# Soft-capped attention for two heads at a time in half-array tiles, with fp32 values and the softmax denominators summed on VectorE

## The chip, the cores and the metric

One core of one Trainium2 chip runs the whole program. The metric is the device time of one execution in microseconds (us). In what follows PE is TensorE, DVE is VectorE, ACT is ScalarE, POOL is GpSimd, and SP is the engine that issues nearly all DMAs.

## The reference

Three layers run one after the other on 4 batches of 448 tokens (12 heads of 64, model width 768):

```python
scores = scale * q @ k.T                       # per head, 448 x 448
scores = cap * np.tanh(scores / cap)
attn = np.exp(scores - max); attn /= attn.sum(-1)
x = (attn @ v)                                 # heads side by side: 1792 x 768
h = x @ w_in                                   # 768 -> 2048, weights given as 64-bit floats
x = (h * np.clip(h + 3, 0, 6) / 6) @ w_out     # 2048 -> 768
# then a top-1 mixture of 8 experts (768 -> 1024 -> 768) with a gate and an output gate
```

All of it is wanted to fp32 accuracy.

## The kernel before

One order of work is written for every engine by a small planner (class `Work`): each step is recorded with its engine, a due time `at`, an assumed duration and the buffers that it uses; `run()` then plays the steps through a list schedule and emits them in the order that it finds. The engines follow that order strictly, each its own, whatever the real times are. DMAs are steps of the engine "sp".

The stages in the order of time: attention of batch 0, with the conversion of the 64-bit weights beside it (`cv`, lines 392 to 446: load, four integer steps on DVE, store to a scratch array); then three stages in each of which the feed-forward layer (`step`, line 640) of batch b runs on PE, and the attention of batch b+1 is woven between its matmuls; the feed-forward layer of batch 3; the experts. In the first of these three stages the rest of the conversion runs too. At the end of each feed-forward layer `route` (line 756) picks the experts, POOL scatters token numbers with four indirect DMAs (line 833, `order<-ids,posi`), and `rows` (line 862) transposes the layer's output back and writes it with the DMA `xs<-spare` (line 885).

Attention is recorded head by head (`head`, line 479). q and k are turned by four PE transposes each pair of key chunks (line 492). ACT copies them out as fp32r, a format that PE multiplies in one pass (line 505); DVE subtracts to get the rounding rests (lines 509, 511). High part and rest lie in different halves of the 128 array rows, so that two matmuls per key chunk give all the products that are kept (lines 554, 555). For this the halves are doubled by two DMAs within the chip per head (line 516, `qk<-qk`; for the first four heads by copies on DVE or ACT). ACT takes tanh (line 561) and exp (line 568). The values:

- heads 0 to 15 (`nat`): one fp32 matmul per key chunk (line 582), shown in the trace as two records;
- the others: exp is split in a high part and a rest (line 300 or 298, and line 575), and three fp32r matmuls per key chunk follow (lines 586 to 588).

In both cases POOL copies v into a wider tile whose other 64 columns are ones (lines 532, 537, 540), so that the same matmul gives the denominators in the other 64 output rows. Four ACT copies per pair of heads bring values and denominators to the right halves (line 600), DVE divides (lines 617 to 625).

The buffers that couple the engines: two tiles each for q2, k2, v2, loaded by SP (line 462); the load of v waits until POOL has copied the older v out. Two raw weight tiles `wr` and three split ones `ws`; two row tiles `spare` for `rows`. PSUM: S0, S1 (two banks each) for scores, T for transposes, U (and F1 in batch 0) for values, F0, F1 for the feed-forward layer.

## Time and profile before

| | us |
|---|---|
| median of 3 runs | 1168.71 (1166.28 to 1173.0) |
| the profiled execution | 1165.38 |
| its span, first to last instruction | 1163.7 |
| attention of batch 0 and feed-forward 0 with attention 1, up to the first routing | 0 to 285 |
| feed-forward 1 with attention 2, up to the second routing | 285 to 480 |
| feed-forward 2 with attention 3, up to the third routing | 480 to 661 |
| feed-forward 3, up to the last routing | 661 to 805 |
| experts | 805 to 1164 |

The ends of the stages are the starts of the routing matmuls (line 778): six fp32 matmuls with 32 output columns each, which stand at four column positions of the array in turn (0, 32, 64, 96, 0, 32), two records each. The page's first part gives each engine's busy time, the second the same by 40 slices of 29 us; the windows give it by stage. A matmul's duration in a record overlaps that of the next one; what one costs in a stream is the distance between two starts.

### The profile page before, as it was taken

Reading aid. Unit: us, or ns where it says so; the run is one execution under the profiler, and the core shown is the slowest. Engines: PE = TensorE matmul, PEld = TensorE weight load, DVE = VectorE, ACT = ScalarE, POOL = GpSimd, SP = SyncE. Lnnn points to the kernel's source line nnn. Section 1 sums busy time; section 2 is a strip of 40 time slices with the busy share of each in tenths; the row PEclk is TensorE's granted clock in tenths of the full one; section 3 lists DMA queues with packets and bytes.
Section 4 is the critical chain, followed back from the end, with each engine's and each line's share of the span. In section 5 each row is a group of like instructions: output and inputs, shape, how many; then the busy total and the mean of one; then the engine's idle time right before and its main releaser. Section 6 shows DMA issues by size and latency. Waiting matters only on the chain.

```text
span 1163.7 us, 17177 instructions
## 1 busy us (share of the span) xinstructions
PE 1067.8 (92%) x5416; PEld 879.7 (76%) x5416; DVE 789.2 (68%) x1317; ACT 763.2 (66%) x1056; POOL 138.5 (12%) x209
## 2 busy tenths in 40 slices
PE   6879999999989999949999987999849999999995
PEld 3446888888879999739999876998746667886764
DVE  6879898997854676726587562444927776886662
ACT  7889877986855886836687352434726766886663
POOL 2001001111120010110013002000171100110001
PEclk9999999999989999979999999999979999999998
DMA  8888888884763443334333287345356868949562
GB/s 246 254 248 237 263 251 250 258 264 128 133 113 113 113 130 95 85 76 143 94 94 102 68 170 205 120 129 211 89 180 220 304 217 310 351 164 333 171 187 82
DMA packets 123985, 209.43 MB, mean 180 GB/s; under 512 B 14010, under 2 KB 82474, under 8 KB 123888
## 3 DMA queue, kind: packets, MB, share of 16 engines
q1 hardware_dynamic: 120304, 197.22, 57.6%
q0 software_dynamic: 3584, 11.04, 2.7%
q8 instruction: 45, 0.74, 0.3%
q14 instruction: 52, 0.43, 0.1%
HBM read 224.20 MB, written 25.83 MB: 215 GB/s over the span
## 4 chain that ended last, share of the span: by engine, by line
PE 50%; DMA 16%; DVE 13%; issue 13%; ACT 4%; POOL 2%; SPq 1%; POOLq 0%; DVEq 0%
PE F L636 8%; PE F L634 8%; PE F L635 8%; PE S L634 5%; PE S L636 4%; PE S L635 4%; DMA order<-ids,posi 4%; DMA xs<-spare 3%; DMA f<-in_moe_w_in_dram 2%; PE F L1387 2%; PE S L554 2%; PE S L555 2%; DVE ws L663 2%; PE U L587 1%; PE U L586 1%
## 5 line engine op out<-in xcount | busy, mean ns | idle before, releaser
L663 DVE TENSOR_TENSOR ws<-wr,ws 128x768 fp32r<-128x768 f32 (+1 forms) x112 | 119.4, 1068 | 75.1 <-ACT ws L660 73.9
L660 ACT ACTIVATE ws<-wr 128x768 fp32r<-128x768 f32 (+1 forms) x112 | 104.2, 931 | 47.6 <-DMA wr<-wsi 24.0
L634 PE MATMUL F<-gT,ws 128*128 128x448 f32 x320 | 119.0, 372 | 1.2 <-ACT ws L660 1.2
L636 PE MATMUL F<-gT,ws 128*128 128x448 f32 x320 | 117.9, 368 | 2.0 <-DVE ws L663 2.0
L635 PE MATMUL F<-gT,ws 128*128 128x448 f32 x320 | 117.1, 366 | 0.0
L561 ACT ACTIVATE S<-S,rcap 112x896 f32<-112x896 f32 x96 | 93.5, 976 | 26.9 <-PE S L555 26.3
L575 DVE TENSOR_TENSOR el<-et,eh 112x896 fp32r<-112x896 f32 x64 | 70.1, 1095 | 24.9 <-ACT eh L300 24.1
L634 PE MATMUL S<-ring,hTm 128*128 128x384 f32 x224 | 83.7, 374 | 0.0
L554 PE MATMUL S<-qk 128*112 128x448 f32 x192 | 80.2, 417 | 1.1 <-DMA qk<-qk 1.0
L634 PE MATMUL F<-xTb,ws 128*128 128x448 f32 x192 | 73.7, 384 | 4.6 <-DVE r L690 3.9
L635 PE MATMUL S<-ring,hTm 128*128 128x384 f32 x224 | 76.4, 341 | 1.1 <-DVE ring L1258 1.1
L636 PE MATMUL S<-ring,hTm 128*128 128x384 f32 x224 | 76.2, 340 | 0.0
L634 PE MATMUL F<-xTa,ws 128*128 128x448 f32 x192 | 74.6, 389 | 1.7 <-DVE r L690 1.2
L1258 DVE TENSOR_TENSOR ring<-w2B,ring 128x768 fp32r<-128x768 f32 x56 | 52.6, 956 | 29.4 <-ACT ring L1254 26.4
L1258 DVE TENSOR_TENSOR ring<-w2A,ring 128x768 fp32r<-128x768 f32 x56 | 52.9, 956 | 28.5 <-ACT ring L1254 27.7
L555 PE MATMUL S<-qk 128*112 128x448 f32 x192 | 71.8, 374 | 0.0
L636 PE MATMUL F<-xTb,ws 128*128 128x448 f32 x192 | 70.8, 369 | 0.0
L635 PE MATMUL F<-xTa,ws 128*128 128x448 f32 x192 | 70.8, 369 | 0.0
L636 PE MATMUL F<-xTa,ws 128*128 128x448 f32 x192 | 70.7, 368 | 0.0
L635 PE MATMUL F<-xTb,ws 128*128 128x448 f32 x192 | 70.7, 368 | 0.0
L1254 ACT ACTIVATE ring<-w2B 128x768 fp32r<-128x768 f32 x56 | 46.9, 846 | 34.9 <-PE S L636 32.3
L568 ACT ACTIVATE et<-S,capt 112x896 f32<-112x896 f32 x64 | 64.4, 1007 | 7.5 <-DVE el L575 6.3
(269 smaller groups left out, 2723.3 us busy)
## 6 DMA issues: line engine op xcount, KB each, us to landing
wr<-wsi SPq DMA_DIRECT2D x64, 384.0 KB
wr<-wso SPq DMA_DIRECT2D x48, 512.0 KB
w1A<-in_moe_w_dram SPq DMA_DIRECT2D x42, 512.0 KB
w2A<-in_moe_w_dram SPq DMA_DIRECT2D x56, 384.0 KB
w1B<-in_moe_w_dram SPq DMA_DIRECT2D x42, 512.0 KB
w2B<-in_moe_w_dram SPq DMA_DIRECT2D x56, 384.0 KB
spare<-in_moe_w_dram SPq DMA_DIRECT2D x72, 256.0 KB
spare<-in_moe_w_dram SPq DMA_DIRECT2D x96, 192.0 KB
```

What stands on the lines that cost most here:

```text
L554: nc.tensor.matmul(out=sp[:P, j, 0:S], lhsT=k1f[:, c], rhs=qsf, start=True, stop=False)
L555: nc.tensor.matmul(out=sp[:P, j, 0:S], lhsT=kkf[:, c], rhs=qsf, start=False, stop=True)
L561: lambda sv=sv: A.activation(out=sv, in_=sv, func=ACTF.Tanh, scale=rcap[:P]), [s] + caps, [hs])
L568: lambda sv=sv, hx=hx: A.activation(out=hx.t, in_=sv, func=ACTF.Exp, scale=capt[:P]), [s], [hs, hx])
L575: lambda e=e, he=he, el=el: V.tensor_tensor(out=el, in0=e, in1=he.t.bitcast(F32), op=ALU.subtract),
L634: nc.tensor.matmul(out=acc, lhsT=lh, rhs=rh, start=first, stop=False)
L635: nc.tensor.matmul(out=acc, lhsT=lh, rhs=rl, start=False, stop=False)
L636: nc.tensor.matmul(out=acc, lhsT=ll, rhs=rh, start=False, stop=last)
L660: lambda: A.activation(out=s[:, 0, 0:n], in_=t, func=ACTF.Copy), [x], [hw, hs])
L663: lambda: V.tensor_tensor(out=s[:, 1, 0:n], in0=t, in1=s[:, 0, 0:n].bitcast(F32), op=ALU.subtract),
L1254: "act", at - 5e3, 40 + w * 0.887, lambda: A.activation(out=hs.t[:, 0, 0:w], in_=raw(), func=ACTF.Copy),
L1258: lambda: V.tensor_tensor(out=hs.t[:, 1, 0:w], in0=raw(), in1=hs.t[:, 0, 0:w].bitcast(F32), op=ALU.subtract),
```

## The change

`head(g)` becomes `pair_qk(n)` and `pair(n)`, for two heads that stand in the two halves of the array.

- q, k, v are loaded with the two heads side by side in each key chunk (pieces of 64 numbers, 256 bytes, where there were 256 numbers); a transpose then turns both heads at once. One ACT copy and one DVE subtraction for each of q and k.
- Scores: three products (high x high, high x rest, rest x high), each as two matmuls, one per head, on 64 array rows each and into banks of their own: six instructions per key chunk and pair, where there were four.
- The doubling of halves is gone, with its DMAs and copies.
- Values in fp32 for all heads: per key chunk two matmuls of 64 output columns, one per head, into the two halves of one bank. v is read as it was loaded; POOL has no part in it.
- Denominators: DVE adds the four exp tiles of a pair (three additions of 112x896), and two fp32 matmuls with ones follow. The high part, rest and copy of exp are gone.
- One ACT copy of the denominators per pair; DVE's division reads the values from PSUM.
- In batch 0 transposes take T and F0 in turn; from batch 1 on scores are recorded for two key chunks at a time.
- The planner's due times: T0 88 to 70, T1 188 to 174, conversions every 4.4 where it was 5.5; six feed-forward matmuls are assumed to take 1225 ns where it was 1125.

```diff
@@ -274,7 +262,7 @@
-    nc.gpsimd.iota(tokid, pattern=[[1, 2], [2, 2]], base=0, channel_multiplier=C, allow_small_or_imprecise_dtypes=True)
+    nc.gpsimd.iota(tokid, pattern=[[1, C]], base=0, channel_multiplier=C, allow_small_or_imprecise_dtypes=True)
...
     Sp, Tp, Up, F, U2 = banks("S0", "S1"), banks("T"), banks("U"), banks("F0", "F1"), banks("U", "F1")
+    T2 = banks("T", "F0")
     TU, Y3 = banks("T", "U"), banks("S0a", "S0b", "S1a", "S1b")
-    QKV = {nm: ring(atp, 2, [P, 2, C, D], nm) for nm in ("q2", "k2", "v2")}
-    QK = ring(atp, 2, [128, 3, 2, 2 * P], "qk", F32R)
-    ET = ring(atp, 1, [P, 2, S], "et")
-    EH = Tag(atp, 3, [P, 2, S], "eh")
-    EL = ring(atp, 2, [P, 2, S], "el", F32R)
+    QKV = {nm: ring(atp, 2, [P, C, 2, D], nm) for nm in ("q2", "k2", "v2")}
+    QK = ring(atp, 2, [128, 2, 2, S], "qk", F32R)
+    EE = ring(atp, 7, [P, 2, S], "ee")
+    ES = ring(atp, 1, [P, 2, S], "es")
...
-    for par in range(2):
...
-    T0, T1, TL = 88e3, 188e3, 120e3
+    T0, T1, TL = 70e3, 174e3, 120e3
...
-        at = i * 5.5e3 if i < 16 else max(T0, t_ff(i // 2) - 30e3)
+        at = i * 4.4e3 if i < 16 else max(T0, t_ff(i // 2) - 30e3)
...
@@ -459,166 +432,137 @@
-                nc.sync.dma_start(
-                    out=h.t.rearrange("p h c d -> p h (c d)"),
-                    in_=src[b, 2 * p:2 * p + 2].rearrange("h (p c) d -> p h (c d)", c=C),
-                )
+                nc.sync.dma_start(out=h.t, in_=src[b, 2 * p:2 * p + 2].rearrange("h (p c) d -> p c h d", c=C))
...
+    def pair_qk(n):
         b, p = divmod(n, H // 2)
...
+        t0, per = t_head(2 * n), (t_head(2 * n + 2) - t_head(2 * n)) / 2
+        load(n)
+        (hq, lq), (hk, lk) = (loaded[n, nm] for nm in ("q2", "k2"))
+        TR = T2 if b == 0 else Tp
+        hw = QK.take()
+        w = hw.t
+        ready = []
+        for i, (h, l) in enumerate(((hq, lq), (hk, lk))):
+            ht = TR.take()
+            def trans(tp=ht.t, t=h.t):
+                for c in range(C):
+                    nc.tensor.transpose(tp[:, c * P:(c + 1) * P], t[:, c].rearrange("p h d -> p (h d)"), ident[:P, :P])
+            at = t0 - 1.6 * per + i * 500
+            tt = ht.t[:, 0:S]
+            x = work.add("pe", at, 392, trans, [l], [ht, h], rows=P)
+            x = work.add(
+                "act", at + 1e3, 467, lambda i=i, tt=tt: A.activation(out=w[:, i, 0], in_=tt, func=ACTF.Copy),
+                [x], [ht, hw])
+            ready.append(work.add(
+                "dve", at + 1e3, 535,
+                lambda i=i, tt=tt: V.tensor_tensor(
+                    out=w[:, i, 1], in0=tt, in1=w[:, i, 0].bitcast(F32), op=ALU.subtract),
+                [x], [ht, hw]))
+        turned_qk[n] = hw, ready
+    def pair(n):
+        b, p = divmod(n, H // 2)
+        t0, per = t_head(2 * n), (t_head(2 * n + 2) - t_head(2 * n)) / 2
+        hv, lv = loaded[n, "v2"]
+        hw, ready = turned_qk[n]
+        w = hw.t
+        TR, UR = (T2, U2) if b == 0 else (Tp, Up)
+        hu, hsum = UR.take(), ES.take()
+        uv, es = hu.t, hsum.t
+        many = 1 if b == 0 else 2
+        et, last = [], None
+        for c0 in range(0, C, many):
+            at = t0 + c0 * per / 2
+            hs = [Sp.take() for _ in range(many)]
+            def score(c0=c0, hs=hs):
+                for c, h in enumerate(hs):
+                    for t, (i, j) in enumerate(((0, 0), (0, 1), (1, 0))):
+                        for r in range(2):
+                            o = slice(64 * r, 64 * r + 64)
+                            nc.tensor.matmul(
+                                out=h.t[:P, r, 0:S], lhsT=w[o, 1, i, (c0 + c) * P:(c0 + c + 1) * P], rhs=w[o, 0, j],
+                                start=(t == 0), stop=(t == 2))
+            s = work.add("pe", at - 0.8 * per, 200 + 612 * many, score, ready, hs + [hw])
+            for c, h in enumerate(hs):
+                sv = h.t[:P, :, 0:S]
+                x = work.add(
+                    "act", at - 4e3 + c * 2e3, 900,
+                    lambda sv=sv: A.activation(out=sv, in_=sv, func=ACTF.Tanh, scale=rcap[:P]), [s] + caps, [h])
+                he = EE.take()
+                x = work.add(
+                    "act", at - 3e3 + c * 2e3, 900,
+                    lambda sv=sv, he=he: A.activation(out=he.t, in_=sv, func=ACTF.Exp, scale=capt[:P]), [x], [h, he])
+                et.append((he, x))
+                k = len(et) - 1
+                if k == 0:
+                    continue
+                one = et[0][0] if k == 1 else hsum
+                last = work.add(
+                    "dve", at - 2e3 + c * 2e3, 1002,
+                    lambda he=he, one=one: V.tensor_tensor(out=es, in0=one.t, in1=he.t, op=ALU.add),
+                    [et[0][1], x, last], [he, one, hsum] if k == 1 else [he, hsum])
+        hd = TR.take()
+        dv = hd.t
+        def pv(c0):
+            for c in range(c0, c0 + 2):
+                for r in range(2):
+                    nc.tensor.matmul(
+                        out=uv[64 * r:64 * r + 64, 0:S], lhsT=hv.t[:, c, r], rhs=et[c][0].t[:, r],
+                        start=(c == 0), stop=(c == C - 1))
+        def total():
+            for r in range(2):
+                nc.tensor.matmul(out=dv[64 * r:64 * r + 64, 0:S], lhsT=ones[:, 0:64], rhs=es[:, r], start=True, stop=True)
+        x = None
+        for c0 in range(0, C, 2):
+            hes = [et[c][0] for c in (c0, c0 + 1)]
+            if c0 + 2 < C:
+                x = work.add(
+                    "pe", t0 + c0 * per / 2, 1700, lambda: pv(0), [et[0][1], et[1][1], lv], [hu, hv] + hes, rows=P)
             else:
...
+                x = work.add(
+                    "pe", t0 + c0 * per / 2, 2450, lambda c0=c0: (pv(c0), total()), [x, et[2][1], et[3][1], last],
+                    [hu, hv, hd, hsum] + hes, rows=P)
+        hx, hy, hr, hc, xt = UX.take(), US.take(), RT.take(), RC.take(), XT[b % 2].take()
         ux, us, rt, rc, x2 = hx.t, hy.t, hr.t, hc.t, xt.t
         nb = S // 32
 
         def blocks(t):
             return t.rearrange("p (n w) -> p n w", w=32)
 
...
+        at = min(t0 + 2.5 * per, T0 + b * T1 - 6e3 + p * 500)
+        pe = x
+        x = work.add("act", at, 467, lambda: A.activation(out=us, in_=dv[:, 0:S], func=ACTF.Copy), [pe], [hd, hy])
+        x = work.add("dve", at, 535, lambda: V.transpose(out=blocks(rt), in_=blocks(us)), [x], [hy, hr])
         x = work.add("dve", at, 160, lambda: V.reciprocal(out=rc, in_=blocks(rt)[:, :, 0:1]), [x], [hr, hc])
         x = work.add(
             "dve", at, 535, lambda: V.transpose(out=blocks(us), in_=rc.to_broadcast([128, nb, 32])), [x], [hc, hy])
...
+        x = work.add(
+            "dve", at, 535, lambda: V.tensor_tensor(out=ux, in0=uv[:, 0:S], in1=us, op=ALU.mult), [x, pe], [hu, hx, hy])
         x = work.add(("dve", "act"), at, (302, 467), copier(x2[:, 0], ux), [x], [hx, xt])
         x = work.add(
             "dve", at, 535,
...
-                "pe", t0 + m / n * (t1 - t0), 1125, mm, [ws, last, xs_[m][1], xs_[m + 1][1]],
+                "pe", t0 + m / n * (t1 - t0), 1225, mm, [ws, last, xs_[m][1], xs_[m + 1][1]],
...
-    plan = [(t_head(g) if g else -1, lambda g=g: head(g)) for g in range(NH)]
-    plan += [(i * 5.5e3 if i < 16 else t_ff(i // 2) - 30e3, lambda i=i: cv(i)) for i in range(len(parts))]
+    plan = [(t_head(2 * n - 2) - 1 if n else -2, lambda n=n: pair_qk(n)) for n in range(NH // 2)]
+    plan += [(t_head(2 * n) if n else -1, lambda n=n: pair(n)) for n in range(NH // 2)]
+    plan += [(i * 4.4e3 if i < 16 else t_ff(i // 2) - 30e3, lambda i=i: cv(i)) for i in range(len(parts))]
     plan += [(t_ff(i), lambda i=i: step(i)) for i in range(len(ff))]
```

What stands on PE in batch 0, before, around the turning of the second pair's first head (T: transposes; S: scores; U: values):

```order
L492 MATMUL T<-ident,q_140 128x112 x2
L492 MATMUL T<-ident,k_142 128x112 x2
L582 MATMUL U<-eh,vf_188 128x448 x2
L554 MATMUL S_133<-qk_146 112x448
L555 MATMUL S_133<-qk_146 112x448
L554 MATMUL S_133<-qk_146 112x448
L555 MATMUL S_133<-qk_146 112x448
L582 MATMUL U<-eh,vf_188 128x448 x2
L554 MATMUL S_134<-qk_146 112x448
L555 MATMUL S_134<-qk_146 112x448
L554 MATMUL S_134<-qk_146 112x448
L555 MATMUL S_134<-qk_146 112x448
```

and now, in the third pair:

```order
L499 MATMUL S_133<-qk_145 112x448 x6
L530 MATMUL U<-ee_148,v_143 64x448 x2
L530 MATMUL U<-ee_149,v_143 64x448 x2
L461 MATMUL F_137<-ident,k_142 128x112 x4
L499 MATMUL S_134<-qk_145 112x448 x6
L499 MATMUL S_133<-qk_146 112x448 x6
L499 MATMUL S_134<-qk_146 112x448 x6
L530 MATMUL U<-ee_150,v_143 64x448 x2
L530 MATMUL U<-ee_151,v_143 64x448 x2
L536 MATMUL T<-es_154,ones 64x448 x2
L499 MATMUL S_133<-qk_146 112x448 x6
```

Full-array transposes, 64-row scores (x6) and 64-column values (x2) now alternate; before, all of them used all rows and columns.

On POOL around the second routing, before (va, vb: copies of v; order: the scatters):

```order
L540 TENSOR_TENSOR vb_193<-v_143,va_192 112x4x64
L537 CAST va_186<-v_144 112x4x64
L540 TENSOR_TENSOR vb_187<-v_144,va_186 112x4x64
L833 DMA order<-ids,posi 14336x1 x4
L537 CAST va_192<-v_144 112x4x64
L540 TENSOR_TENSOR vb_193<-v_144,va_192 112x4x64
L537 CAST va_186<-v_143 112x4x64
```

and now, from the first routing on:

```order
L1089 MEMSET spare 128x1538
L1090 MEMSET spare 112x128
L777 DMA order<-ids,posi 14336x1 x8
L1133 MEMSET xrow_4538 128x769
L1133 MEMSET xrow_4539 128x769
L870 IOTA reach 128x112 x4
```

The copies of v that stood before and behind the scatters are gone; only scatters and, later, set-up for the experts are left.

On SP around the second routing, before (v, q, k: loads; wr: weights; xs: rows):

```order
L885 DMA xs<-spare 112x769
L657 DMA wr_170<-wsi_71 128x768
L462 DMA v_144<-in_v_dram 112x2x256
L516 DMA qk_145<-qk_145 64x2x224 x2
L657 DMA wr_171<-wsi_72 128x768
L657 DMA wr_170<-wso_0_81 128x1024
L885 DMA xs<-spare 112x769
L657 DMA wr_171<-wso_1_82 128x1024
L885 DMA xs<-spare 112x769
```

and now:

```order
L601 DMA wr_175<-wsi_71 128x768
L601 DMA wr_176<-wsi_72 128x768
L829 DMA xs<-spare 112x769
L601 DMA wr_175<-wso_0_81 128x1024
L829 DMA xs<-spare 112x769
L435 DMA q_139<-in_q_dram 112x8x64
L601 DMA wr_176<-wso_1_82 128x1024
L829 DMA xs<-spare 112x769
L601 DMA wr_175<-wso_2_83 128x1024
```

The load of v stood ahead of weights and rows and waited for POOL; the loads now stand among weights and rows, and what frees their tiles is PE.

## Rows read from the trace of the kernel before

**Rows 1.** First part of the page: busy time (share of the span) xinstructions of each engine.
```profile
PE 1067.8 (92%) x5416; PEld 879.7 (76%) x5416; DVE 789.2 (68%) x1317; ACT 763.2 (66%) x1056; POOL 138.5 (12%) x209
```

**Rows 2.** Windows: busy us (xcount) of PE, PEld, DVE, ACT, POOL; granted clock, DMA share, GB/s.
```profile
0.00:120.00 120.00, 94.94 (x360) 62.35 (x361) 94.33 (x203) 100.44 (x141) 15.00 (x42) 0.97 0.85 244
120.00:285.00 165.00, 161.31 (x791) 141.25 (x792) 153.85 (x275) 130.03 (x185) 15.93 (x19) 1.00 0.79 242
```

**Rows 3.** Windows at the first two routings, same columns.
```profile
300.00:330.00 30.00, 25.88 (x134) 22.66 (x132) 19.34 (x35) 17.93 (x29) 2.43 (x3) 1.00 0.93 111
330.00:360.00 30.00, 28.11 (x131) 25.70 (x132) 15.10 (x20) 18.19 (x26) 5.97 (x7) 0.89 0.45 118
480.00:510.00 30.00, 22.88 (x120) 19.86 (x118) 18.25 (x42) 18.36 (x28) 6.12 (x8) 0.97 0.32 55
510.00:540.00 30.00, 20.27 (x94) 18.49 (x95) 15.93 (x24) 13.96 (x20) 1.13 (x2) 0.75 0.54 160
```

**Rows 4.** Timeline of SP at the second routing: start us, us, engine, line, op, names [idle before].
```profile
486.51 0.35 SPq L657 DMA_DIRECT2D wr<-wsi  x1
506.69 0.33 SPq L462 DMA_DIRECT2D v<-in_v_dram  x1
```

**Rows 5.** Waits of the SP queue, 285 to 540 us: us in total, times, longest.
```profile
SPq L462 <- POOL va L537: 20.1, 1, 20.1
SPq L462 <- POOL vb L540: 14.7, 4, 13.2
```

**Rows 6.** Timeline of POOL at the second routing.
```profile
504.51 0.94 POOL L833 DMA_INDIRECT order<-ids,posi  x1 [5.43 <-DMA order<-ids,posi]
505.46 0.40 POOL L537 CAST va<-v 112x256 fp32r<-112x256 f32 x1
```

**Rows 7.** Timeline of DVE at the second routing.
```profile
519.00 0.15 DVE L882 COPY spare<-wt 112x1 f32<-112x1 f32 x1 [19.00 <-DMA xs<-spare]
```

**Rows 8.** Waits of PE, 285 to 540 us.
```profile
PE F L873 <- DVE r L690: 22.2, 3, 16.2
```

**Rows 9.** Timeline of PE in batch 0; xN merges N records.
```profile
47.70 0.36 PE L554 MATMUL S<-qk 128*112 128x448 f32 x1
47.91 0.36 PE L555 MATMUL S<-qk 128*112 128x448 f32 x1
48.11 1.67 PE L582 MATMUL U<-eh,vf 112*128 112x448 f32 x4
```

**Rows 10.** Groups by line and form, 0 to 661 us: busy us, mean ns | idle before.
```profile
L575 DVE TENSOR_TENSOR el<-et,eh 112x896 fp32r<-112x896 f32 x64 | 70.1, 1095 | 24.9 <-ACT eh L300 24.1
...
L511 DVE TENSOR_TENSOR qk<-T,qk 64x224 fp32r<-64x224 f32 x96 | 37.3, 389 | 2.2
...
L582 PE MATMUL F<-eh,vf 112*128 112x448 f32 x48 | 20.3, 546 | 1.4 <-ACT eh L568 1.3
...
L298 DVE CAST eh<-et 112x896 fp32r<-112x896 f32 x27 | 17.2, 638 | 25.5 <-ACT et L568 25.5
...
L625 DVE TENSOR_TENSOR xTa<-ux,xTa 128x448 fp32r<-128x448 f32 x12 | 7.6, 635 | 0.8 <-ACT xTa L300 0.6
```

**Rows 11.** Timeline of PE at the first routing.
```profile
284.67 0.37 PE L636 MATMUL F<-xTb,ws 128*128 128x448 f32 x1
284.96 1.70 PE L778 MATMUL F<-spare,wg 128*32 128x448 f32 x12
286.59 0.47 PE L586 MATMUL U<-eh,va 112*128 112x448 f32 x1
286.90 0.37 PE L587 MATMUL U<-el,va 112*128 112x448 f32 x1
287.10 0.36 PE L588 MATMUL U<-eh,vb 112*128 112x448 f32 x1
```

**Rows 12.** DMA queue, 10 to 11 us: packets, MB, share of 16 engines (small packets).
```profile
q1 hardware_dynamic: 1312, 0.17, 123.8%
```

**Rows 13.** DMA queue, 0 to 285 us, same columns.
```profile
q1 hardware_dynamic: 57920, 69.00, 81.1%
```

More of the change, by code (lines that the diff above doesn't have):

```diff
@@ L66, in take @@
         return h
-class Tag(Ring):
-    def __init__(self, pl, n, shape, nm):
-        Ring.__init__(self, [], n)
-        self.make = lambda dt: pl.tile(shape, dt, tag=nm, name=nm, bufs=n)
-    def take(self, dt):
-        self.turns.append(Held(self, len(self.turns), lambda: self.make(dt)))
-        return self.turns[-1]
 class Work:
@@ L307, in attention_ffn_moe @@
     NH2 = HF // 2
-    NAT = 16
-    NFIRST = 4
-    REST = [2 * (j % 2) + j // 2 for j in range(C)]
     bank, last_turn = {}, {}
@@ L470, in load @@
                 caps.append(work.add("dve", at, 300, cap_parts, [x]))
[L472 to L475 removed]
+    turned_qk = {}
+    def pair_qk(n):
         b, p = divmod(n, H // 2)
[L477 to L609 removed]
@@ L614, in blocks @@
             return t.rearrange("p (n w) -> p n w", w=32)
-        at = min(t0 + 1.5 * per, T0 + b * T1 - 6e3 + p * 500)
-        x = work.add("dve", at, 535, lambda: V.transpose(out=blocks(rt), in_=blocks(us)), uev[n], [hy, hr])
+        at = min(t0 + 2.5 * per, T0 + b * T1 - 6e3 + p * 500)
+        pe = x
+        x = work.add("act", at, 467, lambda: A.activation(out=us, in_=dv[:, 0:S], func=ACTF.Copy), [pe], [hd, hy])
+        x = work.add("dve", at, 535, lambda: V.transpose(out=blocks(rt), in_=blocks(us)), [x], [hy, hr])
         x = work.add("dve", at, 160, lambda: V.reciprocal(out=rc, in_=blocks(rt)[:, :, 0:1]), [x], [hr, hc])
```

127 lines of the change are left out of this document (1 added, 126 removed).

## The prediction

> **What bounds the kernel now.** I read the page's first part, then windows by stage, then the waits and timelines at the places where PE falls short. PE is busy 92% of the span [rows 1], so PE's work and its holes are what counts. Up to the first routing (0 to 285 us) PE has 94.94 + 161.31 = 256.3 us of work and DVE 94.33 + 153.85 = 248.2 [rows 2]: PE is idle 28.7 us, DVE 36.8, and from 120 us on both are over 90% busy, with the DMA engines at 0.79 to 0.85. That stage has two bounds close together. The next two stages (285 to 480, 480 to 661) are PE's alone, except for two holes, one at each routing. The second hole can be followed. PE waits 16.2 us in one piece for DVE [rows 8]; DVE stands 19.0 us before it can fill a row tile whose DMA has not gone [rows 7]; SP's queue does nothing between 486.5 and 506.7 [rows 4], since the load of v waits 20.1 us for POOL's copy of v [rows 5]; and POOL can't copy because four scatters stand ahead of that copy, each waiting for the one before, the last at 504.5 [rows 6]. At the first routing the load of v waits 13.2 us in the same way [rows 5]. The price in PE's windows [rows 3]: idle 4.1 + 1.9 us at the first, 7.1 + 9.7 at the second, and afterwards a granted clock of 0.89 and 0.75 (a mean between full speed, 2.4 GHz, and half), which fell behind the idle time.
>
> **The change part by part.** All sums are made against the profiled execution's 1165.4 us, 0.3% below the median of the three runs shown.
>
> *PE's work.* A 448-column fp32r matmul costs 0.205 us from start to start, an fp32 one two passes: four records last 1.67 us, the last alone 0.55, so (1.67 - 0.55) / 3 = 0.375 a pass [rows 9, 10]. A pair of heads before: 16 score matmuls, 3.28 us; values 8 x 2 x 0.375 = 6.0 in the first 8 pairs, 24 x 0.205 = 4.92 in the other 16. Together 9.28 or 8.20. After: 4 chunks x 3 products, two heads at once, 12 x 0.205 = 2.46 us; values and denominators 10 matmuls, two at once, 5 x 2 x 0.375 = 3.75; together 6.21. Transposes stay as many.
>
> That two tiles run at once is seen for column tiles: the routing's twelve fp32 passes at four column positions take 286.59 - 284.96 = 1.63 us [rows 11], where one after the other they would take 12 x 0.375 = 4.5. For row tiles no row shows it. Bounds for a round of two score matmuls: 0.205 (at once) and 0.41 (in turn). I take 0.205, since the column tiles are the nearest row, and keep 0.41 as a rival.
>
> What the tiles cost beside their passes is seen at the same place: entering, 284.96 - 284.67 - 0.205 = 0.09 us; leaving, 1.63 - 4 x 0.375 = 0.13; and the first full-array matmul behind takes 0.31 to the next start, 0.10 too much [rows 11]. That is 0.32 there and back, 0.16 a change. In the new order PE changes between full array, 64-row and 64-column tiles 177 times: 95 up to the first routing, 38 up to the second, 44 up to the third. The upper bound for one: the overlap of two matmuls is lost (0.36 - 0.205 = 0.16) and one weight load stands open (879.7 us over 5416 loads, 0.16 each [rows 1]), so 0.32.
>
> The Trainium skill speaks against the change here: "TensorEngine Tiling (Array Packing)", section Key Properties, says that a change of tiling mode, not merely of tile, drains the array. The rows on the routing agree that a change costs something, and give it 0.16 us; with a full drain at the 0.32 above, the sum would be 177 x 0.16 = 28 us worse.
>
> Saved on PE: up to the first routing 13 pairs (8 + 5): 74.2 + 41.0 - 80.7 = 34.5, less 95 x 0.16 = 15.2, so 19.3 us. To the second, 5 pairs: 41.0 - 31.1 - 6.1 = 3.9. To the third, 6 pairs: 49.2 - 37.3 - 7.0 = 4.9.
>
> *DVE.* A pair loses eight rests of q and k, 8 x 0.389 = 3.11 us, and gets two of full height, 2 x 0.635, and three additions, 3 x 1.095 for the same form [rows 10]: 4.56. In the first 8 pairs that is 1.45 us more each. In the others four rests of exp (4 x 1.095) and four copies, 27 of 64 on DVE (1.08 a pair), go as well: 4.0 us less each. Up to the first routing: 8 x 1.45 - 5 x 4.0 - 1.9 (five halves doubled on DVE) = 10.3 us less, so 237.9. In batch 0 alone DVE gets more work; there ACT is the busier (100.4 of 120 us [rows 2]), and ACT loses five of its eight copies per pair and the copies of exp. Behind DVE's additions wait the denominators' matmuls, and with them what is queued on PE; before, the rests of exp stood in the same place.
>
> *DMA.* Through 285 us packets cost 0.811 x 285 x 16 / 57920 = 64 ns at 1.19 KB [rows 13], small ones, 130 bytes in the mean, 1.238 x 16 / 1312 = 15 ns [rows 12]. A load goes from 224 packets of 1 KB to 896 of 256 bytes. Between the two rows a 256-byte packet takes 21 ns: 0.4 us of all engines' time more per load, 39 loads, 15 us; the doubling DMAs (22 heads, 44 by then, 128 packets of 896 bytes at some 50 ns each) take back 18. Net near nothing; at 64 ns a packet it would be 90 us more. I take the line between the rows: 256 bytes are near the small end. SP issues 88 DMAs less and waits for PE, not POOL, to free v; behind that wait stand weights and conversions, but values of the pair two before are done by then.
>
> *The holes.* v is read as loaded, POOL has only the scatters, and SP no longer waits for it. What is late next: the scatters' own effect on the DMA engines, which stand at 0.93 busy for 111 GB/s at the first routing [rows 3]. Bounds: nothing gained (the weights are late all the same), or all: 6.0 idle + 0.11 x 30 = 9.3 at the first, 16.9 idle + some 3 of slow clock at the second. At the first I take half, 5: SP's wait there was shorter than the slow stretch. At the second 14 of 16.9: the wait accounts for all but one scatter's time.
>
> *Sum.* Up to the first routing: if PE keeps its 28.7 us of idle time beside 237.0 of work, 19 us are gained; if DVE keeps its 36.8 beside 237.9, 10. I take 15. To the second routing 3.9 + 5 = 9, to the third 4.9 + 14 = 19. The feed-forward layer of batch 3 and the experts have no attention. In all 43: **1122 us**. With each bound on its poorer side (10 + 4 + 5) 1146, on its better (19 + 13 + 25) 1108.
>
> **The rivals.**
> - *The holes stay* (another wait takes the place of POOL's): for it, the DMA rate at the first routing; against it, at the second SP issued nothing at all for 20 us. It takes back 5 + 14: 1141 us.
> - *Changes of mode cost a full drain*, 0.32 us: against it the routing's rows, for it that 64-row tiles stand in no row. 28 us less gain: 1150.
> - *The row tiles run in turn*, so the change does not do what it says for scores: each of 288 rounds takes 0.205 us more, 59 us of PE's work, nearly all on PE's path: 1181, slower than before. It decides from a round of about 0.36 us on (43 / 288 = 0.15 over 0.205). For it only that no row shows 64-row tiles; against it the column tiles, and that the two heads write different banks.
> - *Weight loads don't overlap in column tiles.* If each of the 240 pass rounds bore its load, 0.16 us [rows 1], 39 us more: 1161. Against it, the routing's loads of 32 columns do not show between its passes [rows 11]. The Trainium skill has this as a rule ("TensorE: Matmul & The Clock Gate", Packing small matmuls: a weight load overlaps running matmuls only if its row group differs); by that rule column tiles would get nothing for their loads, and the trace disagrees.
>
> **How the numbers follow.** Chances: forecast 0.62, holes stay 0.17, full drains 0.09, rows in turn 0.08, weight loads 0.02, small packets at the price of large ones 0.02 (slower). The range takes in the sum's better side with some room for holes elsewhere, 1100, and reaches a little past the drains, 1154: what is left out is the serial cases, 0.12, and a little below. 0.5% of the time, about what a measurement of this kernel can tell from no change, is 6 us. Faster by more: 0.62 + 0.17 + 0.09 less a little for sums of two rivals, 0.85; within: 0.05; slower: 0.10.
>
> **What would show it.** In the changed kernel: two score records starting within some 10 ns, and rounds 0.2 us apart; value passes in pairs 0.38 apart; changes of mode of 0.1 to 0.2 us; no wait of SP for POOL before 661 us, and no idle piece of PE over 10 us at the second routing; DVE near 238 us up to the first. Wrong would be scores 0.4 apart, or the first routing later than 280 us (DVE or DMA bound there), or holes of the same size with another releaser.

## The result, and the profile after

The changed kernel takes 1140.93 us (median of 4, 1139.06 to 1141.36) beside 1168.53 for the kernel before: a ratio of 0.9756 [0.9725, 0.9787]. It is faster by some 28 us, and 43 were forecast. Profile against profile it is 1141.21 us (span 1139.5) against 1165.38, 24.2 us less, and the account below is made on these two.

The first part of the page of the changed kernel, busy us (share of the span) and instructions, answers to [rows 1]:

```profile
PE 1050.6 (92%) x5576; PEld 791.5 (69%) x5576; DVE 723.8 (64%) x1145; ACT 661.4 (58%) x900; POOL 81.5 (7%) x123
```

One correction first. The table ahead of the prediction puts the second routing at 480 us and the last at 805; their matmuls begin at 466.3 and 802.7, and the second routing's first scatter goes at 480.9. The hole of the kernel before, from 503 to 519 us, lies behind the start at 466.3, in the third stage, where the sum credited it.

With the stages cut where a routing's matmuls begin, these are the windows of the kernel before and of the changed one. The columns are the stretch and its length, then busy us (instructions) of PE, PEld, DVE, ACT and POOL, the granted clock, the DMA share and GB/s.

```profile
0.00:285.00 285.00, 256.25 (x1150) 203.60 (x1152) 248.18 (x477) 230.47 (x325) 30.92 (x61) 0.99 0.81 243
285.00:466.30 181.30, 175.25 (x885) 157.48 (x884) 118.89 (x205) 126.10 (x178) 19.58 (x26) 0.98 0.50 115
466.30:661.20 194.90, 177.45 (x895) 159.30 (x894) 119.06 (x204) 124.97 (x175) 24.58 (x50) 0.96 0.34 95
661.20:802.70 141.50, 131.34 (x637) 116.00 (x637) 61.77 (x113) 53.96 (x85) 10.89 (x13) 0.96 0.60 163
802.70:1163.70 361.00, 327.53 (x1863) 243.29 (x1862) 241.27 (x322) 227.73 (x293) 52.50 (x59) 0.96 0.64 216
```

```profile
0.00:280.00 280.00, 252.53 (x1314) 168.53 (x1314) 232.75 (x406) 192.85 (x263) 3.40 (x17) 0.96 0.80 231
280.00:447.40 167.40, 163.55 (x863) 128.37 (x865) 90.51 (x149) 88.56 (x124) 5.64 (x4) 0.99 0.43 103
447.40:629.30 181.90, 172.49 (x905) 133.74 (x904) 98.00 (x158) 98.00 (x136) 10.27 (x30) 0.97 0.36 90
629.30:775.10 145.80, 132.41 (x640) 117.28 (x639) 61.16 (x114) 54.12 (x84) 10.37 (x13) 0.95 0.58 159
775.10:1139.50 364.40, 329.63 (x1863) 243.56 (x1862) 241.36 (x322) 227.82 (x293) 51.77 (x59) 0.97 0.64 214
```

| stage | gain | forecast | PE busy | PE idle |
|---|---|---|---|---|
| to the first routing | 5.0 | 15 | 256.3 to 252.5 | 28.8 to 27.5 |
| to the second | 13.9 | 9 | 175.3 to 163.6 | 6.1 to 3.9 |
| to the third | 13.0 | 19 | 177.5 to 172.5 | 17.5 to 9.4 |
| to the fourth (no attention) | -4.3 | 0 | 131.3 to 132.4 | 10.2 to 13.4 |
| to the end | -3.4 | 0 | 327.5 to 329.6 | 33.5 to 34.8 |

**The tiles run at once.** The timeline of PE in the changed kernel (start us, us, engine, line, names, records) answers to [rows 9]:

```profile
325.32 1.47 PE L499 MATMUL S<-qk 64*112 64x448 f32 x12
326.73 0.54 PE L817 MATMUL F<-ident,spare 128*112 128x128 f32 x3
...
384.51 1.72 PE L530 MATMUL U<-ee,v 112*64 112x448 f32 x8
386.17 0.47 PE L578 MATMUL F<-xTb,ws 128*128 128x448 f32 x1
```

Twelve score records, two chunks of two heads, take 1.41 us to the next start: six rounds 0.20 apart, not twelve, of which the first and the last bear some 0.09 more; inside, they start in pairs 3 ns apart. Eight value records take 1.66 us: four passes of 0.375 (pairs 7 ns apart), and 0.16 for getting in and out. Row tiles behave as the column tiles of [rows 11] did.

**The waits at the routings are shorter.** Windows of the changed kernel at the first two routings, as in [rows 3]:

```profile
300.00:330.00 30.00, 26.42 (x139) 21.28 (x139) 16.74 (x28) 17.52 (x27) 3.28 (x3) 0.94 0.74 126
330.00:360.00 30.00, 30.00 (x149) 26.51 (x148) 9.08 (x9) 9.74 (x14) 0.00 (x0) 1.00 0.37 102
450.00:480.00 30.00, 28.02 (x159) 20.91 (x156) 20.85 (x51) 20.52 (x30) 2.96 (x3) 1.00 0.45 76
480.00:510.00 30.00, 22.57 (x110) 17.80 (x108) 14.00 (x22) 10.79 (x18) 0.94 (x1) 0.83 0.55 129
```

The waits of the SP queue from 280 to 540 us, the two longest releasers of L435 (the loads of q, k and v), answer to [rows 5]; the longest wait of PE there answers to [rows 8]:

```profile
SPq L435 <- PE T L461: 41.7, 15, 6.5
SPq L435 <- PE U L530: 20.0, 7, 7.5
```

```profile
PE F L817 <- DVE r L634: 6.9, 1, 6.9
```

No wait for POOL is left: a load of q, k or v waits for PE's transposes and values, 7.5 us at the longest where POOL held one for 20.1. The queue's largest wait in total is for the raw weight tiles, which DVE frees (L601 for L607): 157.5 us in 36 waits, 9.5 at the longest; from 285 to 540 us in the kernel before it was 98.8 in 28. PE's longest wait at the second routing fell from 16.2 to 6.9 us, not to zero.

### The profile page after: what moved, and what is told of

It is laid out like the page before. It is cut to its first block, busy times and chain, and to the rows that moved or that the text cites. A ratio compares the mean times of both kernels' runs of the same rounds, so it can differ in the third digit from the quotient of the medians.

```text
span 1139.5 us, 16743 instructions
## 1 busy us (share of the span) xinstructions
PE 1050.6 (92%) x5576; PEld 791.5 (69%) x5576; DVE 723.8 (64%) x1145; ACT 661.4 (58%) x900; POOL 81.5 (7%) x123
## 4 chain that ended last, share of the span: by engine, by line
PE 58%; DMA 16%; issue 12%; DVE 8%; ACT 4%; POOL 1%; SPq 0%; POOLq 0%; DVEq 0%; ACTq 0%
PE F L578 10%; PE F L579 9%; PE F L580 9%; PE S L578 5%; PE U L530 5%; PE S L580 4%; PE S L579 4%; PE S L499 3%; DMA f<-in_moe_w_out_dram 3%; DMA order<-ids,posi 3%; DMA f<-in_moe_w_in_dram 3%; PE F L1332 2%; DMA xs<-spare 2%; DVE ring L1203 2%; DMA out_dram<-y,tk 1%
## 5 line engine op out<-in xcount | busy, mean ns | idle before, releaser
L607 DVE TENSOR_TENSOR ws<-wr,ws 128x768 fp32r<-128x768 f32 (+1 forms) x112 | 119.5, 1068 | 83.2 <-ACT ws L604 81.1
L508 ACT ACTIVATE S<-S,rcap 112x896 f32<-112x896 f32 x96 | 91.2, 975 | 19.8 <-PE S L499 19.1
L512 ACT ACTIVATE ee<-S,capt 112x896 f32<-112x896 f32 x96 | 94.0, 1012 | 0.3
L499 PE MATMUL S<-qk 64*112 64x448 f32 x576 | 78.1, 399 | 10.4 <-ACT ee L512 5.4
L578 PE MATMUL F<-xTb,ws 128*128 128x448 f32 x192 | 74.9, 390 | 7.3 <-DVE r L634 7.3
L578 PEld LDWEIGHTS F<-gT,ws 128*128 128x128 f32 x320 | 60.1, 188 | 25.6 <-issue 16.8
L530 PE MATMUL U<-ee,v 112*64 112x448 f32 x336 | 77.0, 582 | 0.8 <-DVE ux L565 0.8
L578 PE MATMUL F<-xTa,ws 128*128 128x448 f32 x192 | 75.3, 392 | 2.4 <-DVE r L634 0.9
L631 ACT ACTIVATE r<-F,three 128x448 f32<-128x448 f32 x64 | 40.5, 633 | 63.1 <-PE F L580 62.6
L499 PEld LDWEIGHTS S<-qk 64*112 64x112 f32 x576 | 48.4, 181 | 36.5 <-issue 13.9
L579 PE MATMUL F<-xTb,ws 128*128 128x448 f32 x192 | 71.4, 372 | 0.0
L580 PE MATMUL F<-xTb,ws 128*128 128x448 f32 x192 | 71.2, 371 | 0.0
L579 PE MATMUL F<-xTa,ws 128*128 128x448 f32 x192 | 70.8, 369 | 0.0
```

The costliest lines, as they stand in the source:

```text
L499: nc.tensor.matmul(out=h.t[:P, r, 0:S], lhsT=w[o, 1, i, (c0 + c) * P:(c0 + c + 1) * P], rhs=w[o, 0, j], start=(t == 0), stop=(t == 2))
L508: lambda sv=sv: A.activation(out=sv, in_=sv, func=ACTF.Tanh, scale=rcap[:P]), [s] + caps, [h])
L512: lambda sv=sv, he=he: A.activation(out=he.t, in_=sv, func=ACTF.Exp, scale=capt[:P]), [x], [h, he])
L530: nc.tensor.matmul(out=uv[64 * r:64 * r + 64, 0:S], lhsT=hv.t[:, c, r], rhs=et[c][0].t[:, r], start=(c == 0), stop=(c == C - 1))
L578: nc.tensor.matmul(out=acc, lhsT=lh, rhs=rh, start=first, stop=False)
L579: nc.tensor.matmul(out=acc, lhsT=lh, rhs=rl, start=False, stop=False)
```

## The experiments

Twelve kernels ran in four groups, each group on one chip beside the kernel before, whose median was 1173 to 1177 us there and not 1168.5. So ratios are compared; the changed kernel's own is 0.976. Runs a_... change the changed kernel, b_... the kernel before; line numbers in a run's rows are those of its own kernel. The stages are those of the table above, in us, from the profiled execution.

| run | median | ratio to before | stages 1 to 5 |
|---|---|---|---|
| (changed) | 1140.9 | 0.976 [0.973, 0.979] | 280.0, 167.4, 181.9, 145.8, 364.4 |
| a_router | 1147.1 | 0.977 [0.973, 0.981] | 283.5, 172.7, 182.4, 144.9, 363.1 |
| a_poolv | 1173.9 | 1.000 [0.997, 1.003] | 284.0, 183.7, 194.2, 146.7, 364.9 |
| b_v3 | 1177.1 | 1.001 [0.998, 1.004] | 289.7, 183.9, 197.5, 140.8, 366.1 |
| b_plan | 1199.6 | 1.019 [1.013, 1.025] | 292.3, 205.6, 197.3, 144.4, 362.4 |
| a_plan0 | 1152.1 | 0.983 [0.979, 0.986] | 286.6, 179.7, 177.2, 142.1, 361.9 |
| a_1125 | 1149.4 | 0.977 [0.973, 0.981] | 283.8, 165.0, 186.6, 142.3, 364.7 |
| a_t1 | 1167.2 | 0.991 [0.987, 0.995] | 281.5, 182.2, 185.1, 146.1, 366.8 |
| a_t166 | 1157.0 | 0.987 [0.984, 0.991] | 279.7, 177.1, 181.1, 147.1, 362.8 |
| a_f64x3 | 1147.7 | 0.975 [0.969, 0.981] | 270.2, 182.5, 184.7, 146.9, 362.5 |
| b_f64x3 | 1193.3 | 1.014 [1.008, 1.020] | 284.2, 204.5, 197.8, 139.3, 366.8 |
| a_fill | 1163.5 | 0.990 [0.986, 0.994] | 284.5, 187.4, 182.9, 152.2, 364.7 |
| a_padd | 1181.3 | 1.003 [1.000, 1.006] | 295.8, 182.8, 181.2, 148.5, 365.1 |

The profiled execution lies 4 to 7 us from the median in b_plan, a_1125, a_t1, a_t166 and a_padd, and 10 in a_fill. A stage is read where it differs by more than 5 us, or where several kernels agree.

### Do row tiles need alternating order? (a_router)

```diff
-                    for t, (i, j) in enumerate(((0, 0), (0, 1), (1, 0))):
-                        for r in range(2):
+                    for r in range(2):
+                        for t, (i, j) in enumerate(((0, 0), (0, 1), (1, 0))):
```

> The changed kernel with the score matmuls of a chunk in another order: all three of the upper head, then all three of the lower, the same 576. If two row tiles run at once only where instructions that follow each other lie in different halves, a chunk takes 4 to 6 rounds of 0.20 us instead of 3, that is 19 to 58 us more TensorE time over 96 chunks, some two thirds of it on the path: 1154 to 1180. If each half had a queue of its own and ran ahead, 1140 to 1146 and a visit of twelve would stay at 1.41 us.

The time is the changed kernel's, and so is the visit. PE's timeline in this run:

```profile
334.49 1.48 PE L499 MATMUL S<-qk 64*112 64x448 f32 x12
335.90 0.55 PE L817 MATMUL F<-ident,spare 128*112 128x128 f32 x3
```

If matmuls began strictly in the order written, upper three then lower three, only the last of one triple could run beside the first of the next: at least nine rounds for twelve, 1.8 us and more. It is again 1.41 to the next start, six rounds. So the halves don't wait for each other, at least three matmuls deep, and the rival "in turn" is gone in both orders. As this kernel does the same work in the same order but for that, it stands for the changed kernel on the chip of its group (1147.1 us) in comparing the next one, a_plan0 and a_fill. By the ratio 0.976 the changed kernel would be at 1145 us there.

### Is it GpSimd in front of the load of v? (a_poolv, b_v3)

a_poolv puts a copy by GpSimd back between v's load and the values:

```diff
+    VC = ring(atp, 2, [P, C, 2, D], "vc")
...
-        hv, lv = loaded[n, "v2"]
+        h0, l0 = loaded[n, "v2"]
+        hv = VC.take()
+        lv = work.add("pool", t0 - per, 973, lambda: G.tensor_copy(out=hv.t, in_=h0.t), [l0], [h0, hv])
```

> The changed kernel, but GpSimd again copies each pair's v (into one of two tiles that the value matmuls read), as the kernel before did with its split, so that the load of a later v waits for GpSimd once more. Hole theory: the waits of the SP queue for GpSimd come back at the routings (10 to 20 us each, one to three of them), TensorE idles beside them, and the second and third stage become 5 to 15 us longer each: 1150 to 1170. Rival: the holes went because TensorE and VectorE have less to do there, wherever v comes from: 1139 to 1146, with no wait over 3 us of TensorE beside them.

It is as slow as the kernel before: 26.8 us over a_router, nearly all in the second and third stage (11.0 and 11.8). Waits of the SP queue and of PE between 284 and 662 us:

```profile
SPq L436 <- POOL vc L483: 35.3, 5, 21.0
```

```profile
PE F L581 <- DVE spare L286: 28.3, 4, 20.8
```

The mechanism is confirmed: a copy of 0.86 us a pair, on an engine that is idle nearly everywhere, costs as much as the change gained, since behind scatters it holds the queue from which v, weights and rows go. It also shows that the terms don't add: this kernel has the cheaper matmuls, PE is busy 596.7 us up to its third routing beside 609.0 before, and that gain stood as idle time (65 us beside 52) and as a lower granted clock (0.93, 0.96 and 0.95 in the three stages, where the kernel before had 0.99, 0.98 and 0.96). Whether freeing the queue alone, with the old matmuls, would gain anything no run shows; the next one was to try it.

b_v3 tried the opposite, a third tile for v in the kernel before:

```diff
-    QKV = {nm: ring(atp, 2, [P, 2, C, D], nm) for nm in ("q2", "k2", "v2")}
+    QKV = {nm: ring(atp, 3 if nm == "v2" else 2, [P, 2, C, D], nm) for nm in ("q2", "k2", "v2")}
```

> The kernel before, with a third tile for v, so that SP's load of v need not wait for POOL's copy behind the scatters. Theory H (the holes at the first two routings are POOL's wait passed on by SP): SP's waits of 13.2 and 20.1 us for POOL go, PE's wait of 16.2 us at the second routing shrinks below 6, time 1145 to 1155. Rival D (the DMA engines are slow under the scatters whatever SP does): the holes keep over two thirds of their size, 1160 to 1168.

No gain. Its SP queue, whole span:

```profile
SPq L462 <- POOL va L537: 22.9, 1, 22.9
```

PE's longest wait at the second routing is 16.6 us, where it had 16.2. At 517 us 23 loads of v have gone where in the kernel before 22 had at 507, each behind GpSimd's work on the same head (the 40th): the planner uses the third tile to send a load one pair earlier, and the load that is held behind the scatters is just the next one. More room doesn't take away the wait; another reader of v does.

### What are the planner's numbers worth? (b_plan, a_plan0, a_1125, a_t1, a_t166)

b_plan gives the kernel before the change's four numbers, a_plan0 the changed kernel the old four:

```diff
-    T0, T1, TL = 88e3, 188e3, 120e3
+    T0, T1, TL = 70e3, 174e3, 120e3
...
-        at = i * 5.5e3 if i < 16 else max(T0, t_ff(i // 2) - 30e3)
+        at = i * 4.4e3 if i < 16 else max(T0, t_ff(i // 2) - 30e3)
...
-                "pe", t0 + m / n * (t1 - t0), 1125, mm, [ws, last, xs_[m][1], xs_[m + 1][1]],
+                "pe", t0 + m / n * (t1 - t0), 1225, mm, [ws, last, xs_[m][1], xs_[m + 1][1]],
...
```

> The kernel before with the change's planner numbers alone (T0 70, T1 174, conversions every 4.4, six feed-forward matmuls at 1225 ns); the work is the old one. If the gain is from less work and the freed POOL: no gain, 1163 to 1175. Rival: the retimed order itself brings it, 1145 to 1155.

> The changed kernel with the four planner numbers of the kernel before (88 and 188 us for the heads, 5.5 us between conversions, 1125 ns for a feed-forward group). If the numbers carry part of the gain: 1146 to 1165, the loss in the first three stages. If the edit of the attention alone carries it: 1137 to 1145. The 4 us that the fourth stage (third to fourth routing, no attention in it) is longer than in the kernel before come from the numbers if it goes back from 145.8 to about 141, and not if it stays.

In the kernel before the new numbers cost 1.9%, some 22 us: the same waits, now at both routings and longer. The waits of PE and of the SP queue in b_plan, beside 22.2 us and one wait of 20.1 in the kernel before [rows 5, 8]:

```profile
PE F L873 <- DVE r L690: 43.7, 2, 25.2
```

```profile
SPq L462 <- POOL va L537: 49.2, 2, 25.3
```

With the old numbers the changed kernel is 5.0 us slower than a_router and keeps some 21 of its 26 us (1152.1 beside 1147.1 and 1173.6). So the edit carries the gain. The numbers add some 5 us to it by this comparison and 8 by the ratios (0.983 for 0.976), with intervals that just touch; without the edit they lose.

a_1125, a_t1 and a_t166 change one number of the changed kernel: the group's 1225 back to 1125, or T1 from 174 to 188 and to 166.

> The changed kernel with one planner number of the kernel before, the 1125 ns of a feed-forward group (the change has 1225). If that number makes the fourth stage (no attention) longer and the third too, they fall from 145.8 and 182 to about 142 and 177 with the first two as in the changed kernel: 3 to 8 us faster than the changed kernel on the same chip, a ratio to the kernel before of 0.968 to 0.974. If the gain in those two stages came from the spacing of the heads, or is paid for earlier: a ratio of 0.974 to 0.982.

> The changed kernel with one other planner number of the kernel before, 188 us of heads for each batch after the first (the change has 174). If the spacing sets the third and fourth stage: those fall to about 177 and 142, and the second grows from 168 towards 180, a ratio to the kernel before of 0.972 to 0.982. If it is the group's 1225 that sets them, third and fourth stay at 182 and 146.

> The changed kernel with the heads of each batch after the first spaced over 166 us and not 174 (188 in the kernel before, and with that one number the changed kernel lost 17 us in its second and third stage). Spacing theory: the plan's spacing is the pace of those stages, and both shorten by up to 8 us each: a ratio to the kernel before of 0.962 to 0.970. Work theory: 336 of the 350 us of the two stages are TensorE busy already, no spacing takes that away: a ratio of 0.972 to 0.982, with the second and third stage together 343 to 356 us.

The fourth stage follows the group's number: 142.1 and 142.3 us in the two variants with 1125, 144.9 to 152.2 in the changed kernel and its seven variants with 1225; with the old attention it is 139.3 to 141.5 in the three kernels with 1125, and 144.4 in b_plan. That is where its 4.3 us went. But a_1125 is not faster (0.977): in its profile the first and third stage are longer by 3.8 and 4.7. T1 is worse to either side, mostly in the second stage (182.2 and 177.1 beside 167.4, and 172.7 in a_router): there neither "the spacing is the pace" nor "PE's work is fixed, so nothing changes" was right. In a_t166 PE did less by the first routing (1281 records to 279.7 us beside 1314 to 280.0, the scores of 13 pairs beside 14) and had it left over. Each number sets an order, and none of these orders beats the one chosen.

### What bounds the way to the first routing? (a_f64x3, b_f64x3, a_fill, a_padd)

In the trace of the changed kernel each load of a conversion (L385) goes when the last integer step (L402) of the conversion two before has ended; SP waits there 76.7 us in all. A third tile relieves that:

```diff
-    F64 = ring(atp, 2, [128, NH2, 128, 2], "f64", I32)
+    F64 = ring(atp, 3, [128, NH2, 128, 2], "f64", I32)
```

> The changed kernel with a third tile for the 64-bit weights that are converted (two before). Theory L: up to the first routing the pace is the conversion's loop of two tiles, since a tile's next load is issued when the last integer step on it ends (56 conversions, about 4.6 us each, in both kernels); with three tiles the first routing's matmuls start near 265 us (now 280.0), where PE's work of 237 us with its idle time ends, and the time is 1122 to 1130. Rival P: the stage is bound by PE's or DVE's work as it stands; a third tile moves nothing, 280 and 1138 to 1143.

> The kernel before, with a third tile for the 64-bit weights. Theory L: here too the loop sets the pace, but DVE has 248 us of work up to the first routing and stands close behind, so less is gained than in the changed kernel: first routing 275 to 280 us (now 285.0), time 1158 to 1164. Rival P: no change, 285 and 1165 to 1170.

The theory was half right. In a_f64x3 the first routing comes at 270.2 us instead of 280.0, and the second stage gives it all back. PE's groups of score records up to the first routing, in the changed kernel and in a_f64x3:

```profile
L499 PE MATMUL S<-qk 64*112 64x448 f32 x336 | 48.6, 414 | 10.4 <-ACT ee L512 5.4 <-DVE qk L471 3.5 <-ACT qk L467 1.4
```

```profile
L499 PE MATMUL S<-qk 64*112 64x448 f32 x312 | 47.1, 424 | 16.8 <-ACT ee L512 8.2 <-DVE qk L471 4.7 <-ACT qk L467 3.9
```

At 24 records a pair that is 14 pairs and 13. What came earlier was the routing, not the work. In the kernel before the third tile moved loads so that the hold by GpSimd struck twice (45.7 us): slower.

a_fill adds useless matmuls in the first batch, to see whether PE's lower clock there costs time:

```diff
+        def extra():
+            for _ in range(5):
+                nc.tensor.matmul(
+                    out=dv[:P, 0:S], lhsT=w[:, 1, 0, 0:P], rhs=w[:, 0, 0], start=True, stop=True)
+        more = []
+        if b == 0:
+            for f in (0.3, -0.7):
+                more.append(work.add("pe", t0 - f * per, 1025, extra, ready, [hd, hw]))
...
-                    "pe", t0 + c0 * per / 2, 2450, lambda c0=c0: (pv(c0), total()), [x, et[2][1], et[3][1], last],
+                    "pe", t0 + c0 * per / 2, 2450, lambda c0=c0: (pv(c0), total()), [x, et[2][1], et[3][1], last] + more,
```

> The changed kernel with useless work added to TensorE in the first batch alone: twice for each of its six pairs, five full-array 448-column matmuls (1.03 us at full clock) into the bank of the denominators, ahead of those, 12 us in all. Clock theory (the first stage fell short because TensorE ran at a lower granted clock, .89 through 90 us): the clock of 0 to 90 us rises to .95 or more, and the time is 1135 to 1143, the added work paid by the faster clock. Work theory (the clock is no limit there, or doesn't rise): the clock stays near .89 and the time is 1144 to 1153.

The windows through 90 us of the kernel before, the changed one and a_fill:

```profile
0.00:90.00 90.00, 67.28 (x240) 41.23 (x240) 68.22 (x154) 73.41 (x103) 10.59 (x35) 0.96 0.86 245
```

```profile
0.00:90.00 90.00, 69.45 (x350) 32.80 (x352) 70.52 (x131) 66.96 (x87) 3.40 (x17) 0.89 0.84 225
```

```profile
0.00:90.00 90.00, 73.66 (x365) 37.61 (x366) 63.61 (x117) 61.51 (x80) 3.41 (x17) 0.92 0.78 207
```

The clock rose by 0.03 only: the intervention hardly moved it, and it does not settle what the clock costs. The 12 us of added work cost 16, but not where they were added. Beside a_router the first stage of the profile is 1.0 us longer, the second 14.7 and the fourth 7.3. The planner had twelve steps more to place, so another order may be behind that loss, and it isn't shown that PE's time in the first batch is paid for.

a_padd takes the sums of the exponentials of the first batch from VectorE:

```diff
                 last = work.add(
-                    "dve", at - 2e3 + c * 2e3, 1002,
-                    lambda he=he, one=one: V.tensor_tensor(out=es, in0=one.t, in1=he.t, op=ALU.add),
+                    *(("pool", at - 2e3 + c * 2e3, 3100) if b == 0 else ("dve", at - 2e3 + c * 2e3, 1002)),
+                    lambda he=he, one=one, on=G if b == 0 else V: on.tensor_tensor(
+                        out=es, in0=one.t, in1=he.t, op=ALU.add),
```

> The changed kernel with the sums of the exponentials of the first batch's six pairs made on GpSimd, which is idle there, and not on VectorE: 18 adds of 1.09 us leave VectorE, about 19.5 us of its 70 us busy through 90 us, for an estimated 3.1 us each on GpSimd (894 ns for 256 columns in the kernel before). VectorE theory (it sets the pace of the first batch, TensorE idles 20 of 90 us behind it and loses clock): the first batch ends 8 to 15 us earlier, the granted clock of 0 to 90 us rises above .92 and the time is 5 to 12 us under the changed kernel's on the same chip, a ratio to the kernel before of 0.965 to 0.972. Chain theory (TensorE waits for a pair's chain of steps, whoever makes them; the adds are only slower on GpSimd): a ratio of 0.974 to 0.985.

Both theories missed: some 32 us slower than the changed kernel by the ratios, and VectorE was relieved of nothing (70.6 us busy through 90 us, 70.5 in the changed kernel). Timelines of POOL and DVE in this run:

```profile
42.51 2.31 POOL L520 TENSOR_TENSOR es<-es,ee 112x896 f32<-112x896 f32 x1 [10.06 <-ACT ee L512]
```

```profile
42.79 2.25 DVE L396 TENSOR_SCALAR cva<-f 128x384 int32<-128x384 int32 x1
...
46.48 0.35 DVE L396 TENSOR_SCALAR cva<-f 128x384 int32<-128x384 int32 x1
```

An integer step of 0.35 us took 2.25 and ended 0.2 us behind GpSimd's add. Its sixteen through 90 us took 1020 ns in the mean beside 352 in the changed kernel, the sixteen of L402 973 beside 551; that is 17 us more, where the adds had taken 20. The Trainium skill has it ("SBUF — State Buffer", Who interferes with whom): VectorE and GpSimd share a pair of ports as a lock, and where an instruction of each needs it, whoever comes first holds it for the whole instruction. The rows agree, and the expectation should have reckoned with it. So whether VectorE paces the first batch was not tested. The order of the planner changed here too, and how much of the 32 us is the lock's isn't shown.

## Why the prediction was partly wrong

**PE's terms held in size.** Rounds, passes and changes of tile are as the sum had them: 0.20, 0.375, and a visit of eight value records bears 0.16 us beside its four passes, 0.09 ahead of them and 0.10 at the matmul behind: 0.35 there and back, where 0.32 was taken. Take granted clock times busy time to the second routing: before 256.25 x 0.99 + 175.25 x 0.98 = 425.4, after 252.53 x 0.96 + 163.55 x 0.99 = 404.3, so 21.1 us of work less at full clock (within some 2, by the rounding of the clock); 19.3 + 3.9 = 23.2 were reckoned, and by then both kernels have scored 18.5 pairs. In the third stage PE is busy 5.0 us less, for 4.9, but part of that is clock: at full clock it is 177.45 x 0.96 - 172.49 x 0.97 = 3.0. All three rivals that priced the tiles higher (full drains, rows in turn, open weight loads) are out.

**The first stage was the mis-sized term: 15 became 5.** PE's busy time fell by 3.7 us where 19.3 were reckoned (of which the sum took 15, for DVE's sake), its idle time by 1.3. Two things account for some 12 of the 15.6 missing; the rest is open.
- The routing is no fence for attention. By it the kernel before had scored 13 pairs and taken the values of 12.5, the changed one 14 and 13.5, where the sum had 13 of each in both. A pair's scores (2 x 1.41) and half of its values (1.66) more now are 4.5 us, and half of a pair's values less before are 2.5: some 7 us that the account by stages moves to the second, which gained 13.9 for 9. The first two together gave 18.9 for 24. a_f64x3 shows the same at 10 us: a date moved and no work done.
- The granted clock. Through 90 us PE runs at 0.89 where it had 0.96. An estimate from these numbers, 69.45 x 0.89 / 0.96 = 64.4, puts 5 us of its busy time down to the clock. The sum took every duration at the clock of the kernel before. The lower clock goes with the new attention: through 90 us the four kernels with the old one have 0.96 to 0.98, the ten with the new 0.78 to 0.92. And it goes with a later first routing: in the six of these whose first batch has the same matmuls, additions, weight tiles and due times (changed, a_t166, a_t1, a_router, a_1125, a_poolv) clocks of 0.89, 0.89, 0.89, 0.87, 0.85 and 0.83 stand beside 280.0, 279.7, 281.5, 283.5, 283.8 and 284.0 us. But no run sets the clock alone. The windows of 40 to 50 us show one fall, in the kernel before and in the changed one:

```profile
40.00:45.00 5.00, 2.23 (x10) 1.25 (x9) 4.92 (x13) 4.92 (x7) 0.00 (x0) 0.89 0.97 272
45.00:50.00 5.00, 5.00 (x14) 2.85 (x13) 4.86 (x13) 3.79 (x6) 0.10 (x1) 0.76 0.79 238
```

```profile
40.00:45.00 5.00, 2.30 (x16) 1.10 (x14) 5.00 (x9) 4.68 (x7) 0.00 (x0) 0.88 0.98 271
45.00:50.00 5.00, 4.79 (x16) 2.06 (x18) 4.65 (x10) 4.02 (x5) 0.00 (x0) 0.50 0.39 122
```

Behind equally thin work (2.23 and 2.30 us busy of 5) the clock is 0.76 before and 0.50, all at 1.2 GHz, after. Why it falls further isn't shown; half-array tiles are one thing that differs, and a_fill could not decide it.

**DVE and DMA came out near what was reckoned.** DVE was busy 232.8 us up to the first routing for 237.9 forecast. The 256-byte pieces did what the line between the rows said: 43008 packets of that size (48 loads, where 39 were reckoned) took 19 ns each in the mean, for 21. There are 84272 packets where there were 57920 [rows 13], and the DMA share stayed (0.80 for 0.81):

```profile
q1 hardware_dynamic: 84272, 64.41, 79.7%
```

**The holes: the mechanism right, the size too large.** 5 + 14 were credited and 2.2 + 8.0 of idle time went. With POOL out, what is late next at the second routing is the write of a row tile itself. PE's L817, which turns the layer's output back into rows, waits 6.9 us for DVE, and DVE stands 6.40 us at L826, until an older write has left the tile. That write in the changed kernel (its last copy, its DMA, and DVE behind it):

```profile
476.22 0.55 DVE L286 COPY spare<-F 112x384 f32<-112x384 f32 x1
476.80 0.33 SPq L829 DMA_DIRECT2D xs<-spare  x1
489.77 0.15 DVE L826 COPY spare<-wt 112x1 f32<-112x1 f32 x1 [6.40 <-DMA xs<-spare]
```

and the one in the kernel before that held DVE until 519.00 [rows 7]:

```profile
496.30 0.49 ACT L300 ACTIVATE spare<-F 112x384 f32<-112x384 f32 x1
509.84 0.37 SPq L885 DMA_DIRECT2D xs<-spare  x1
```

Now the write goes as its last copy ends, and the tile is free 13.0 us later. Before, it went 13.0 us behind that copy, which was SP's hold, and the 9.2 us from there to 519.00 were the write's own. The prediction put the whole 19.0 us of DVE's wait down to a DMA that had not gone, and so credited 14 of 16.9. It did name the scatters' load on the DMA engines as late next, but left 2.9 for it; whether the scatters make the write that long no run shows. The rival "the holes stay" gave 1141 us, which is the time measured, but not its mechanism: 10.2 us of idle time went. Where the holes do stay, in a_poolv, the whole gain goes and not the 19 us that the rival was priced at.

**Stages without attention were priced at nothing and cost 7.7.** The fourth lost 4.3 to the planner's 1225, as a_plan0 and a_1125 show; a number that sets an order is not free where the edit itself has nothing to do. The 3.4 of the last stage is within what it varies between these kernels (361.0 to 366.8), and no cause is given.

Of the signs named beforehand all those for the forecast came true: pairs 3 ns apart, rounds of 0.20, passes of 0.375, changes of some 0.17, no wait of SP for POOL, no idle piece of PE over 10 us at the second routing (6.9), DVE near 238 us (232.8). Of those against it, "the first routing later than 280 us" is met on its edge, at 280.0.

Sum: 15 - 5.0, 9 - 13.9, 19 - 13.0, 4.3 and 3.4 make the 18.8 between 43 and 24.2.

## What to carry to other kernels

Before an engine that is idle nearly everywhere is called free, look at what stands ahead of its instruction in its queue, and who waits for it: here a copy of less than a microsecond, put back behind a chain of scatters, took away all that the change had gained. And ask of a wait for a DMA how much of it was spent before the DMA went: only that part goes with what held its queue. Where stages overlap, count what is done by a date (pairs, records) and not the date, and ask what the savings are worth if the changed work is granted a lower clock. Numbers of a planner are part of an edit: the same four gained 5 to 8 us with it and lost 22 without.
